# The zeros for unit 2's k and v change engines, and with them the place in the load queue that waits

## The chip, the cores and the metric

The kernel runs on one core of one Trainium2 chip. The metric is the device time of one execution in microseconds. Five engines run side by side, each with its own instruction stream: PE (matrix products, with a separate row PEld for its weight loads), DVE, ACT, POOL, and SP, which here only issues DMA transfers. SP issues them strictly in program order; an issue that must wait for a semaphore holds up every issue behind it.

## The reference

Eight batches, eight heads, 576 positions, head width 64. First an attention without a score matrix, then a layer that sends 128 of the 576 rows of each batch through an MLP:

```python
q_s = softmax(q over the head width);  k_s = softmax(k over the positions)
kv  = einsum('bhsd,bhse->bhde', k_s, v)
x   = einsum('bhsd,bhde->bhse', q_s, kv)        # heads side by side: (8, 576, 512)

scores = x @ w_gate
for each batch b:
    top = the 128 rows with the highest scores
    h   = max(x[b, top] @ w1, 0)                # 512 -> 1024
    out[b, top] = x[b, top] + sigmoid(scores[b, top]) * (h @ w2)
all other rows: out = x
```

## The kernel before

The attention is done in 16 **units**: unit u is four heads of one batch, two units to a batch. For a unit, ACT takes the exponential of k (`k_exp`, L235, tile `ke`) and of q (`q_exp`, L243, tile `qe`), an engine copies v beside a column of ones (`v_copy`, L247, tile `v_ones`; for unit 2 on POOL, for unit 3 on DVE), PE multiplies them (`kv_mm`, L259), DVE scales the result (`kv_out`), PE transposes q (`q_t`, L289 and L296), ACT or DVE brings it back (L299, L301), PE makes the rows of x (`x_mm`, L321), and DVE scales them (`x_scale`, L339). The scores of a batch are ranked on DVE (`compare`, L389), the 128 rows are found, and the MLP follows (L501 is its first product, in `mlp1`, L510 its second). For batch 0 the rows are not fetched from memory but picked by PE out of the tile that DVE has just written (`select`, L455); the picked rows come back through one copy on ACT (`turned`, L482, tile `xT`), and `mlp1` of batch 0 reads that copy.

The order of the whole program is written out by hand, so each engine's stream is the order of the calls. Raw k, v and q have three buffers each (`LD = 3`), so units 0, 1 and 2 load into fresh buffers and unit 3 takes over unit 0's.

A load of a unit's k or v is two transfers, because the 576 positions are split over 128 partitions, 5 rows to an even partition and 4 to an odd one. `load` (L108) first issues the transfer for the odd partitions (4 rows, 256 KB), then the one for the even partitions (5 rows, 320 KB). The fifth row of the odd partitions is never loaded; a fresh buffer needs zeros there. The zeros are written over the fifth row of all 128 partitions, so the second transfer of the pair writes over part of them and must wait until they are in place; the first does not touch them and does not wait. A load of q is two transfers of 288 KB.

At the start SP issues the loads of units 0 and 1, then unit 2's k, then unit 2's v and q, then w1 in four transfers (L145), then unit 3's k, v and q. POOL writes the zeros of unit 1's k and v and of unit 2's k right after its constants (L207). The zeros of unit 2's v are written by DVE, behind its copy of unit 0's transposed q (L299) and ahead of its half of unit 1's v copy (L793):

```python
q_t(0, 0, on_vector=True)
nc.vector.memset(raw["v"][2][:, :, N2], 0.0)
load(2, "vq")
load_w1(0)
```

Of the kernel before, what the change touches and what calls it, by code (L numbers as in the profile page):

```python
# [17 lines left out]
def kernel(  # L18
# [23 lines left out]
    nc = tc.nc  # L42
# [4 lines left out]
    N2 = R - 1  # L47
# [43 lines left out]
    def place(b):  # L91
        return (b - 1) % B
# [4 lines left out]
    def rows_of(b, upward):  # L97
# [7 lines left out]
    raw = {w: [const.tile([P, 2, T, D] if w == "q" else [P, 4, R, D], F32, name=f"{w}{n}") for n in range(LD)]  # L105
           for w in "qkv"}

    def load(u, which, queues=(nc.sync, nc.sync)):  # L108
        b, qd = units[u]
        for what in which:  # L110
            src = {"q": q, "k": k, "v": v}[what]
            t = raw[what][u % LD]
            first = src[place(b), 4 * qd].offset
            if what == "q":
                for h in range(2):
                    queues[h].dma_start(out=t[:, h].rearrange("p r d -> p (r d)"),
                                        in_=bass.AP(tensor=src.tensor, offset=first + 2 * h * SD,
                                                    ap=[[T * D, P], [1, T * D]]))
                continue
            for n, rows in ((1, N2), (0, R)):  # L120
                queues[n].dma_start(
                    out=t[n::2, :, :rows].rearrange("p h r d -> p h (r d)"),
                    in_=bass.AP(tensor=src.tensor, offset=first + n * R * D,
                                ap=[[T * D, 64], [SD, 4], [1, rows * D]]))
# [16 lines left out]
    def load_w1(half):  # L141

        c = slice(half * F // 2, (half + 1) * F // 2)
        for d in range(0, KD, 2):
            nc.sync.dma_start(out=w1[:, d:d + 2, c],  # L145
                              in_=moe_w1[d * P:(d + 2) * P, c].rearrange("(d p) f -> p d f", p=P))
# [56 lines left out]
    whole = const.tile([P, B * R], I32, name="whole")  # L203
    rest = const.tile([P, B * R], I32, name="rest")
    nc.gpsimd.iota(whole.rearrange("p (b r) -> p b r", b=B), pattern=[[S, B], [1, R]], base=0, channel_multiplier=T)
    for n, what in ((1, "k"), (1, "v"), (2, "k")):
        nc.gpsimd.memset(raw[what][n][:, :, N2], 0.0)  # L207
    load(1, "kvq")
    load(2, "k")
    vals = const.tile([P, B, R, NV], BF16, name="vals")  # L210
    valid_r = const.tile([P, 3, R], F32, name="valid_r")
    s_all = const.tile([P, B, R], F32, name="s_all")
# [63 lines left out]
    def q_t(u, c, on_vector=False, wide=False):  # L276

        if c == 0:
            st["qT", u] = at.tile([P, 2, R, 2, D], F32, tag="qT", name="qT", bufs=1)
        qe = st["qe", u] if c == 0 else st.pop(("qe", u))  # L280
        r0, r1 = ROWS[c]
        n = r1 - r0
        t_ps = ps.tile([P, 2, 512], F32, tag="x", name="x", bufs=2)
        to = st["qT", u][:, :, :n, c]
        if wide:
            to = to.rearrange("p a r t -> p r a t")
            src = t_ps.rearrange("p a c -> p (a c)")[:, :n * P]
            for r in range(n):
                nc.tensor.transpose(out=src[:, r * P:(r + 1) * P], in_=qe[:, r0 + r].rearrange("p i d -> p (i d)"),  # L289
                                    identity=ident)  # L290
            src = src.rearrange("p (r a t) -> p r a t", r=n, a=2)
        else:
            src = t_ps[:, :, :n * D].rearrange("p a (r t) -> p a r t", r=n)
            for r in range(n):
                for a in range(2):
                    nc.tensor.transpose(out=src[:, a, r], in_=qe[part(a), r0 + r].rearrange("p i d -> p (i d)"),  # L296
                                        identity=ident[part(a), part(a)])
        if on_vector:
            nc.vector.tensor_copy(out=to, in_=src)  # L299
        else:  # L300
            nc.scalar.copy(out=to, in_=src)  # L301
# [513 lines left out]
    fill(3)  # L815

    q_t(0, 0, on_vector=True)
    nc.vector.memset(raw["v"][2][:, :, N2], 0.0)
    load(2, "vq")
    load_w1(0)  # L820
    load_w1(1)
    q_t(0, 1)
# [305 lines left out]
```

## Time and profile before

| | |
|---|---|
| median of three runs | 199.6 us (199.15 to 199.66) |
| the profiled execution, its own time | 198.6 us |
| its span, first to last instruction | 196.9 us |
| PE busy | 185.4 us, 94% |
| DVE, ACT, POOL busy | 130.5, 102.7, 71.2 us |
| share of the chain that ended last: PE | 89% |
| share of the chain that ended last: DMA, DVE, ACT | 3%, 3%, 1% |
| moved by DMA | 46.68 MB, mean 237 GB/s |

All rows are of the one profiled execution; its own time is 1.7 us more than its span. Times inside it count from the start of the span. A row of the timeline gives start, duration, engine, line and operation, and in brackets how long the engine had been idle before and what ended that. A row that begins with SPq is a DMA issue: its duration is the time that SP takes to issue, not the time of the transfer. How long a transfer took from issue until it had landed is in the lists of DMA issues, where some engine waited for it.

### The profile page before, as it was taken

The numbers are of one execution on the slowest core, as the hardware profiler recorded it, in microseconds if no ns is written. First come the engines' busy times: TensorE is split into PE (matmuls) and PEld (weight loads), VectorE is DVE, ScalarE is ACT, GpSimd is POOL, SyncE is SP. The second block draws the span as 40 slices with busy tenths as digits, with TensorE's granted clock in tenths as the row PEclk, the third lists the DMA queues.
The fourth block names the chain that finished last, engine by engine and source line by source line (L and its number), as shares of the span: only waits on it lengthen the run. The fifth ranks groups of instructions, "written<-read, shape, count | busy, mean of one in ns | idle before, by whom it ended". The sixth has DMA issues, their size and how long they took to land.

```text
span 196.9 us, 7154 instructions
## 1 busy us (share of the span) xinstructions
PE 185.4 (94%) x2988; PEld 157.7 (80%) x2988; DVE 130.5 (66%) x423; ACT 102.7 (52%) x168; POOL 71.2 (36%) x126
## 2 busy tenths in 40 slices
PE   5799999999999999999999999999999999999950
PEld 2367799984679996679999988899999889898850
DVE  6376967493679659838997987289958955444010
ACT  3265543756597859848675858375433132312100
POOL 8022540201930490099706313145005354701230
PEclk9999999999999999999999999999999999999997
DMA  5999999999999999989968888938341414110011
GB/s 159 336 378 342 357 376 375 359 384 372 377 374 377 361 327 312 340 226 349 280 235 234 299 232 264 283 128 232 118 123 53 123 27 146 44 55 2 3 59 61
DMA packets 35210, 46.68 MB, mean 237 GB/s; under 512 B 2401, under 2 KB 28001, under 8 KB 35170
## 3 DMA queue, kind: packets, MB, share of 16 engines
q1 hardware_dynamic: 33616, 41.62, 64.8%
q0 software_dynamic: 1280, 4.20, 6.6%
q8 instruction: 25, 0.41, 0.8%
q10 hardware_dynamic: 274, 0.33, 0.5%
q14 instruction: 15, 0.12, 0.2%
HBM read 34.61 MB, written 11.53 MB: 234 GB/s over the span
## 4 chain that ended last, share of the span: by engine, by line
PE 89%; DMA 3%; DVE 3%; ACT 1%; issue 1%; POOLq 0%; POOL 0%; DVEq 0%
PE mm L594 19%; PE mm L646 19%; PE x L321 11%; PE tp L259 11%; PE mm L501 8%; PE mm L510 7%; PE x L296 5%; DMA v<-in_v_dram 3%; PE mm L455 2%; PE tp L378 2%; PE x L476 2%; DVE qT L299 1%; PE x L289 1%; PE mm L800 1%; PE tp L414 0%
## 5 line engine op out<-in xcount | busy, mean ns | idle before, releaser
L389 DVE SCALAR_TENSOR_TENSOR junk<-srow,s,stairs 128x576 bf16<-128x576 f32 x40 | 35.9, 897 | 1.3 <-ACT srow L381 0.5
L301 ACT COPY qT<-x 128x512 f32<-128x512 f32 (+1 forms) x30 | 17.9, 642 | 24.2 <-PE x L296 22.8
L339 DVE TENSOR_TENSOR xs<-x,qrec 128x640 f32<-128x640 f32 x32 | 25.2, 814 | 0.0
L439 POOL DMA_INDIRECT xr<-out_dram,idx x8 | 8.1, 1011 | 45.2 <-DVE no L432 14.7
L243 ACT ACTIVATE qe<-q 128x640 f32<-128x640 f32 (+1 forms) x32 | 20.3, 688 | 7.4 <-DMA q<-in_q_dram 7.4
L259 PE MATMUL tp<-v_ones,ke 128*64 128x65 f32 x640 | 22.2, 224 | 1.4 <-DVE v_ones L247 1.2
L321 PEld LDWEIGHTS x<-kv_w,qT 64*64 64x64 f32 x1152 | 20.5, 134 | 3.7 <-ACT qT L301 1.2
L321 PE MATMUL x<-kv_w,qT 64*64 64x66 f32 x1152 | 22.8, 222 | 0.4 <-DVE qT L299 0.4
L235 ACT ACTIVATE ke<-k 128x1280 f32<-128x1280 f32 x16 | 20.4, 1276 | 4.4 <-DMA k<-in_k_dram 4.0
L259 PEld LDWEIGHTS tp<-v_ones,ke 128*64 128x64 f32 x640 | 20.0, 137 | 3.3 <-issue 1.9
L646 PE MATMUL mm<-w,hT 128*128 128x256 f32 x96 | 22.2, 380 | 0.0
L646 PEld LDWEIGHTS mm<-w,hT 128*128 128x128 f32 x96 | 17.8, 191 | 2.1
L594 PE MATMUL mm<-xT,w 128*128 128x128 f32 x144 | 17.5, 276 | 0.0
L646 PE MATMUL mm<-tw,hT 128*128 128x256 f32 (+1 forms) x80 | 17.5, 363 | 0.0
L501 PE MATMUL mm<-xT,w 128*128 128x128 f32 x128 | 17.2, 283 | 0.0
L594 PEld LDWEIGHTS mm<-xT,w 128*128 128x128 f32 x144 | 16.8, 192 | 0.1
L501 PEld LDWEIGHTS mm<-xT,w 128*128 128x128 f32 x128 | 15.2, 192 | 0.8
L510 PE MATMUL mm<-w,hT 128*128 128x512 f32 x32 | 15.6, 611 | 0.0
L655 POOL TENSOR_TENSOR o<-o,xr 128x256 f32<-128x256 f32 x9 | 6.8, 757 | 23.7 <-ACT o L654 23.7
L646 PEld LDWEIGHTS mm<-tw,hT 128*128 128x128 f32 x80 | 13.8, 190 | 1.9 <-DVE o L659 0.3
L247 ACT COPY v_ones<-v 128x1280 f32<-128x1280 f32 x12 | 15.1, 1260 | 0.0
L332 DVE RECIPROCAL qrec<-x 128x10 f32<-128x10 f32 x32 | 7.0, 218 | 10.0 <-PE x L321 9.3
(146 smaller groups left out, 304.6 us busy)
## 6 DMA issues: line engine op xcount, KB each, us to landing
q<-in_q_dram SPq DMA_DIRECT2D x32, 288.0 KB, 5.9
v<-in_v_dram SPq DMA_DIRECT2D x16, 320.0 KB, 5.8
out_dram<-xs SPq DMA_DIRECT2D x16, 320.0 KB, 5.9
k<-in_k_dram SPq DMA_DIRECT2D x15, 320.0 KB, 7.6
k<-in_k_dram SPq DMA_DIRECT2D x16, 256.0 KB, 5.3
v<-in_v_dram SPq DMA_DIRECT2D x16, 256.0 KB
out_dram<-xs SPq DMA_DIRECT2D x16, 256.0 KB, 5.4
w<-in_moe_w_dram SPq DMA_DIRECT2D x4, 512.0 KB, 7.3
```

What stands on the lines that cost most here:

```text
L235: nc.scalar.activation(out=ke, in_=raw["k"][u % LD], func=AF.Exp)
L243: nc.scalar.activation(out=st["qe", u][:, r0:r1], in_=qr[:, r0:r1], func=AF.Exp)
L247: copy(out=v_ones[:, :, :, :D], in_=raw["v"][u % LD])
L259: nc.tensor.matmul(out=kv[part(h), i], lhsT=ke[:, 2 * h + i, r], rhs=vo[:, 2 * h + i, r], start=(r == 0), stop=(r == N2))
L301: nc.scalar.copy(out=to, in_=src)
L321: nc.tensor.matmul(out=to[:, r * C:(r + 1) * C], lhsT=lhsT, rhs=kw[part(i), a], start=True, stop=True)
L339: nc.vector.tensor_mul(xs[b][:, :, qd, :, a].rearrange("p r i d -> p i r d"), x[:, :, :, :D], rec.to_broadcast([P, 2, R, D]))
L389: nc.vector.scalar_tensor_tensor(junk, st["srow", b], st["s", b][:, r:r + 1], not_before[r], op0=OP.subtract, op1=OP.is_ge, accum_out=st[" ...
L501: nc.tensor.matmul(out=h_ps[:, f % HT * m:(f % HT + 1) * m], lhsT=w1[:, d, f * P:(f + 1) * P], rhs=xT[:, d, :m], start=(d == 0), stop=(d = ...
L510: nc.tensor.matmul(out=st["y", b][:m], lhsT=st["hT", b][:, f // HT, f % HT, :m], rhs=w2[:, f], start=(f == 0), stop=(f == KF - 1))
L594: nc.tensor.matmul(out=out_ps[:, f * m:(f + 1) * m], lhsT=w[:, k, f * P:(f + 1) * P], rhs=x()[:, k], start=first and f == 0 and k == 0, st ...
L646: nc.tensor.matmul(out=ps_of[to][:m, c:c + step], lhsT=st["hT", a][:, n, f, :m], rhs=w[:, f, c:c + step], start=first and f == 0, stop=f = ...
```

## The change

The two sets of zeros for unit 2 change places. POOL writes those of unit 2's v at the start instead of those of unit 2's k, and DVE writes those of unit 2's k behind unit 0's transposes instead of those of v. Unit 2's k, whose load was issued with unit 1's, is issued in one call with v and q, which stands behind DVE's zeros in the program.

```diff
-    for n, what in ((1, "k"), (1, "v"), (2, "k")):
+    for n, what in ((1, "k"), (1, "v"), (2, "v")):
         nc.gpsimd.memset(raw[what][n][:, :, N2], 0.0)
     load(1, "kvq")
-    load(2, "k")
...
     q_t(0, 0, on_vector=True)
-    nc.vector.memset(raw["v"][2][:, :, N2], 0.0)
-    load(2, "vq")
+    nc.vector.memset(raw["k"][2][:, :, N2], 0.0)
+    load(2, "kvq")
     load_w1(0)
```

On SP the order of the transfers stays as it was. This is the place in its stream from the last transfer of unit 1's q to the loads of unit 2's q, with what each issue waits for (k_81 and v_84 are unit 2's buffers; a DMAHW wait is for the landing of an earlier transfer; Pool and DVE are the zeros):

```order
 L116 DMA q_77<-in_q_dram 128x576 [waits DMAHW4_49]
 L121 DMA k_81<-in_k_dram 64x4x256 [waits DMAHW5_49]
-L121 DMA k_81<-in_k_dram 64x4x320 [waits DMAHW6_49,Pool_49]
-L121 DMA v_84<-in_v_dram 64x4x256 [waits DMAHW7_49]
-L121 DMA v_84<-in_v_dram 64x4x320 [waits DMAHW0_49,DVE_49]
+L121 DMA k_81<-in_k_dram 64x4x320 [waits DMAHW6_49,DVE_49]
+L121 DMA v_84<-in_v_dram 64x4x256 [waits DMAHW7_49]
+L121 DMA v_84<-in_v_dram 64x4x320 [waits DMAHW0_49,Pool_49]
 L116 DMA q_78<-in_q_dram 128x576 [waits DMAHW1_49]
```

The issue that waits for DVE's zeros is now two transfers further ahead: the second transfer of unit 2's k instead of the second of its v.

## Rows read from the trace of the kernel before

**Rows 1.** The page, its part on the chain of work that ended last: the share of the span by engine.
```profile
PE 89%; DMA 3%; DVE 3%; ACT 1%; issue 1%; POOLq 0%; POOL 0%; DVEq 0%
```

**Rows 2.** The waits of PE from 27 us to the end of the span, all that the view has: who waited for whom, us in total, times, longest.
```profile
PE mm L594 <- DVE xc L567: 0.3, 1, 0.3
```

**Rows 3.** The timeline of SP: the two transfers of unit 2's k, the two of its v; and, after the dots, the second transfer of unit 3's k.
```profile
8.94 0.61 SPq L121 DMA_DIRECT2D k<-in_k_dram  x1
9.70 0.61 SPq L121 DMA_DIRECT2D k<-in_k_dram  x1
10.38 0.60 SPq L121 DMA_DIRECT2D v<-in_v_dram  x1
13.03 0.60 SPq L121 DMA_DIRECT2D v<-in_v_dram  x1
...
18.66 0.76 SPq L121 DMA_DIRECT2D k<-in_k_dram  x1
```

**Rows 4.** The timeline of DVE: the zeros of unit 2's v, the first compare of batch 0, the copy of unit 3's v.
```profile
12.73 0.27 DVE L818 MEMSET v<- 128x256 f32 x1
...
21.66 0.82 DVE L389 SCALAR_TENSOR_TENSOR junk<-srow,s,stairs 128x576 bf16<-128x576 f32 x1
...
29.30 0.83 DVE L247 COPY v_ones<-v 128x1280 f32<-128x1280 f32 x1 [1.42 <-DMA v<-in_v_dram]
```

**Rows 5.** Stretches of the span from the first byte to 15 us: busy time of each engine, granted TensorE clock (1.00 is 2.4 GHz), DMA share, GB/s. No byte is moved before 2 us.
```profile
2.00:13.00 11.00, 9.35 (x91) 4.37 (x95) 6.03 (x34) 4.87 (x7) 2.74 (x7) 1.00 0.98 333
13.00:13.50 0.50, 0.50 (x48) 0.50 (x44) 0.47 (x1) 0.50 (x1) 0.42 (x1) 1.00 1.10 364
13.50:15.00 1.50, 1.50 (x56) 1.01 (x50) 1.32 (x6) 0.88 (x2) 0.60 (x1) 1.00 1.13 355
```

**Rows 6.** The page, its part on DMA issues: size of one transfer, median us from issue to landing.
```profile
q<-in_q_dram SPq DMA_DIRECT2D x32, 288.0 KB, 5.9
v<-in_v_dram SPq DMA_DIRECT2D x16, 320.0 KB, 5.8
...
k<-in_k_dram SPq DMA_DIRECT2D x16, 256.0 KB, 5.3
```

**Rows 7.** The timeline of SP: the first transfer of the program, and two issues later in it that came when the queue had run low.
```profile
0.81 0.76 SPq L121 DMA_DIRECT2D k<-in_k_dram  x1
...
102.51 0.63 SPq L350 DMA_DIRECT2D out_dram<-xs  x1
...
121.50 0.63 SPq L350 DMA_DIRECT2D out_dram<-xs  x1
```

**Rows 8.** Stretches of 0.25 us behind those issues, columns as in rows 5.
```profile
2.75:3.00 0.25, 0.25 (x2) 0.10 (x1) 0.25 (x3) 0.20 (x1) 0.25 (x1) 1.00 0.46 143
3.00:3.25 0.25, 0.25 (x2) 0.05 (x1) 0.25 (x1) 0.25 (x1) 0.25 (x1) 1.00 1.05 348
...
103.50:103.75 0.25, 0.25 (x5) 0.25 (x4) 0.25 (x1) 0.00 (x0) 0.25 (x1) 1.00 0.00 0
103.75:104.00 0.25, 0.25 (x5) 0.25 (x4) 0.03 (x1) 0.19 (x1) 0.24 (x2) 1.00 0.66 164
...
122.00:122.25 0.25, 0.25 (x3) 0.22 (x2) 0.00 (x0) 0.25 (x2) 0.25 (x1) 1.00 0.50 181
...
122.75:123.00 0.25, 0.25 (x3) 0.22 (x2) 0.00 (x0) 0.00 (x0) 0.25 (x1) 1.00 0.76 197
```

**Rows 9.** DMA issues of three short stretches (0 to 1 us, 11 to 13.6 us, 18.7 to 19.4 us), one transfer each: the first transfer of the program, the second of unit 2's v, the second of unit 3's k; size, us to landing.
```profile
k<-in_k_dram SPq DMA_DIRECT2D x1, 256.0 KB, 3.3
...
v<-in_v_dram SPq DMA_DIRECT2D x1, 320.0 KB, 4.7
...
k<-in_k_dram SPq DMA_DIRECT2D x1, 320.0 KB, 9.0
```

**Rows 10.** The timeline of ACT: the exponentials of unit 2's k and q and of unit 3's k, the copy of batch 0's picked rows, the exponentials of unit 3's q.
```profile
17.40 1.27 ACT L235 ACTIVATE ke<-k 128x1280 f32<-128x1280 f32 x1
...
21.43 1.26 ACT L243 ACTIVATE qe<-q 128x640 f32<-128x640 f32 x2
...
27.70 1.27 ACT L235 ACTIVATE ke<-k 128x1280 f32<-128x1280 f32 x1 [2.60 <-DMA k<-in_k_dram]
28.88 0.57 ACT L482 COPY xT<-mm 128x512 f32<-128x512 f32 x1
...
31.23 1.26 ACT L243 ACTIVATE qe<-q 128x640 f32<-128x640 f32 x2 [1.79 <-DMA q<-in_q_dram]
```

**Rows 11.** The timeline of PE: the product of unit 0's k and v, that of unit 2's, the first product of batch 0's MLP, the product of unit 3's k and v, the transposes of unit 3's q.
```profile
9.26 0.36 PE L259 MATMUL tp<-v_ones,ke 128*64 128x65 f32 x5 [1.23 <-DVE v_ones L247]
...
20.84 1.39 PE L259 MATMUL tp<-v_ones,ke 128*64 128x65 f32 x40
...
29.64 2.26 PE L501 MATMUL mm<-xT,w 128*128 128x128 f32 x16
31.83 1.39 PE L259 MATMUL tp<-v_ones,ke 128*64 128x65 f32 x40
33.15 0.78 PE L296 MATMUL x<-ident,qe 64*128 64x64 f32 x18
```

**Rows 12.** The timeline of POOL: the copy of unit 2's v, and the first step on batch 0's scores.
```profile
17.94 1.25 POOL L247 COPY v_ones<-v 128x1280 f32<-128x1280 f32 x1 [3.84 <-DVE qT L299]
20.18 0.20 POOL L361 TENSOR_TENSOR s<-s_all,valid_r 128x5 f32<-128x5 f32 x1 [0.98 <-DVE s_all L359]
```

## The prediction

> **What bounds the kernel now.** I read the chain of work that ended last first, since it says which engine carries the end: 89% of the span is PE [rows 1]. Then the waits of PE: from 27 us to the end there is one, of 0.3 us [rows 2]. So PE is full for the last 170 us, and whatever makes PE late by some time near 30 us comes out at the end whole; no later gap is there to take it up. The question is therefore narrow: does the change make PE late before or around 30 us, and by how much? The change touches only loads and zeros, so the next views are SP's stream [rows 3], the stretches with their GB/s [rows 5], and then, for each load that gets later, who reads it and when [rows 10 to 12].
>
> In the stretches the DMA is the busy thing: from the first byte at 2 us it moves 333 GB/s up to 13 us and 355 to 364 behind that, at a DMA share of about 1 [rows 5]. Loads come in one queue in one order, so a load is late by what the stream ahead of it lost. ACT does wait for it: unit 3's k exponential starts at 27.70 after 2.60 us idle, released by a DMA [rows 10]. The transfer it waits for was issued at 18.66 [rows 3] and took 9.0 us [rows 9]: landed at 27.66. That is the place at which a late stream is felt.
>
> **The change part by part.** *The zeros.* One memset on POOL and one on DVE stay one each, of the same shape; the row of DVE's is 0.27 us [rows 4]. Cost nothing; no other work is moved on either engine.
>
> *The wait on SP.* In the kernel before, SP issues both transfers of unit 2's k at 8.94 and 9.70 and the first of its v at 10.38; the second of its v needs DVE's zeros, which end at 12.73 + 0.27 = 13.00, and it goes out at 13.03 [rows 3, 4]. SP stands still from 10.98 to 13.03, 2.05 us. With the change the second transfer of k has that wait: SP stands still from 9.55 to 13.03, 3.48 us, and what is queued behind it is unit 2's v and q, w1, unit 3's k, v and q, and all later loads. Two transfers, 320 KB of k and 256 KB of v [rows 6], are thus issued 3.3 us later; everything behind them is late at SP by two issue times, 1.2 us. What counts is not SP but whether the DMA engines run out of bytes.
>
> *Do they run dry?* Bytes issued up to and with the first transfer of unit 2's k: two units of k, v and q, each 256 + 320 + 256 + 320 + 288 + 288 = 1728 KB [rows 6], and 256 KB: 3712 KB, which is 3.80 MB. Bytes moved by 13.00: 333 GB/s x 11 us = 3.66 MB; the remaining 0.14 MB takes 0.38 us at 364 GB/s [rows 5]. So the engines are out of work at 13.38 on the mean. In the kernel before, 0.59 MB more was in the queue there, enough at 355 to 364 GB/s until 15.0, and the transfer issued at 13.03 was in time; that stall of SP cost nothing.
>
> *When do bytes flow again?* The issue comes at 13.03. The nearest rows are two later issues at a queue that had run low: issued at 102.51, nothing moved up to 103.75 and 164 GB/s in the next quarter; issued at 121.50, down to 181 GB/s at 122.00 to 122.25 while the old work ran out, and back to 197 from 122.75 [rows 7, 8]. Both are 1.25 us from issue to bytes. So bytes flow from 14.28, and the stream has lost 14.28 - 13.38 = 0.90 us. The cold start is the upper bound: issued at 0.81, still 143 GB/s in the quarter before 3.00 and 348 behind it [rows 7, 8]; 2.2 us, which here means 15.2 and a loss of 1.85 us. The lower bound is no loss, for engines that are still busy when the new work comes. I take 0.90 us, since the two later rows are of a running program.
>
> The Trainium skill's page "DMA: Bandwidth & Descriptors", section "Specifications", gives about 0.6 us to the first byte of a transfer issued from SP, where the rows above show 1.25. By the page the loss would be an estimated 0.25 us, PE would be late by 0.1, and the median would come out at 199.7; the sum goes by the rows.
>
> *Who feels 0.9 us.* Unit 2's k: issued at 13.03 into an empty queue, 3.3 us (the first transfer of the program) to 4.7 us (the one issued at 13.03 now) to landing [rows 9], so 16.3 to 17.7. Its exponential starts at 17.40 now; even if it starts at 17.8 it ends at 19.1, 1.7 us before PE's product at 20.84 needs it [rows 10, 11]. Covered. Unit 2's v lands at 13.03 + 4.7 = 17.73 now; POOL copies it at 17.94 for 1.25 us [rows 9, 12]. At 0.9 us later it ends at 20.1, ahead of the same product at 20.84 and of POOL's own next step at 20.18: covered, with 0.1 us to spare on POOL and another 1.0 us before DVE's compare at 21.66 [rows 4, 12] needs that step's result. Unit 2's q is read at 21.43 with no wait shown [rows 10], and w1 lies ahead of unit 3's k in the queue and is read only behind it. Covered.
>
> Unit 3's k is not. ACT starts its exponential at 27.70 when it lands, and right behind it in ACT's stream stands the copy of batch 0's picked rows, 28.88 to 29.45; PE's first MLP product reads that copy and starts at 29.64 [rows 10, 11]. With k 0.9 us later the exponential starts at 28.60, the copy runs from 29.78 to 30.35, and PE, some 0.05 us behind it, starts at 30.40 instead of 29.64. The slack was 0.14 us, so **0.76 us, say 0.8**, is lost on PE. The copy itself has its data by then; it is late because it is queued on ACT behind a load that is late.
>
> The two behind it are hidden in that: unit 3's v, copied on DVE from 29.30 (also waiting for DMA), would end at 31.0 against a product at 31.83 + 0.8; unit 3's q exponentials, from 31.23 for 1.26 us, would end at 33.4 against transposes at 33.15 + 0.8 [rows 4, 10, 11]. A pause of PE of 0.8 us does not bring the clock down as far as this trace tells: PE idled 1.23 us before 9.26 [rows 11], and the granted clock of that stretch is 1.00, its 2.4 GHz level [rows 5].
>
> *The sum.* Span 196.9 + 0.8 = 197.7 us; the profiled execution 198.6 + 0.8 = 199.4 us; the median of the runs, which lies 1.0 us above the profiled execution, 199.6 + 0.8 = **200.4 us**.
>
> **The rivals.** *First, the last engines never run dry (not slower).* Its place is the queue between 13.0 and 14.3, its price nothing, and its point is 0.14 us: a loss at unit 3's k below that is taken up by the slack at PE's 29.64. What speaks for it: the engines do not run out together. At 122 us the rate falls from 181 GB/s over at least half a microsecond [rows 8], so those that are behind have work to about 0.5 us past the mean, 13.9, and lose 0.4 us; and a transfer has landed only when the last of its engines is done. If the same ones are still last at unit 3's k, the loss there is 0.4 us or less and PE's 0.25 or less. That gives 199.6 to 199.9 us. Against it: nothing shows that the same engines stay last over the 14 us in between.
>
> *Second, a quick restart.* If bytes flow within 0.5 us of the issue at 13.03, the loss is 13.53 - 13.38 = 0.15 us, no more than PE's slack, and the median stays at 199.6. Both later issues speak against it with 1.25 us [rows 7, 8]; for it, only that they were stores and no loads. The page of the Trainium skill named above comes close to it.
>
> *Third, the restart is as slow as at the start.* Loss 1.85 us, PE late by 1.85 - 0.14 = 1.7 us: 201.3 us. Unit 2's v would then end its copy near 21.0, 0.2 us past PE's 20.84, and POOL's scores step would reach DVE's compare just in time, so that place would still add nothing. For it speaks only the cold first transfer [rows 7, 8]; against it, both later issues.
>
> *Fourth, faster.* Nothing on PE's path gets shorter: no load is issued earlier and no instruction goes. It could only be engines that fall into step after running dry, so that later transfers land sooner; PE waits for none of them now [rows 2], so even that buys nothing. What is left is the scatter.
>
> **How the numbers follow.** Forecast 200.4 us: 0.54. First rival, 199.6 to 199.9: 0.26. Second, 199.6: 0.06. Third, 201.3: 0.10. Faster: 0.04. The range goes from 199.5, which takes in the first two rivals and a little scatter, to 201.3, the upper bound of the loss. A measurement of this kernel can tell about 0.3%, or 0.6 us, from no change. The forecast lies only 0.2 us beyond that, so of its 0.54 some 0.12 falls below the line: slower by over 0.3% has 0.42 + 0.10, and with a little scatter from the first rival 0.53; within 0.3% has 0.12 + 0.26 + 0.06 less that scatter, 0.43; faster 0.04.
>
> **What would show it.** In the profile of the changed kernel SP should issue one transfer of unit 2's k near 8.9, the next near 13.0, and unit 2's v behind that. The GB/s should fall in the quarters between 13.2 and 14.3; if they stay above 340 the engines never ran dry and the first rival holds. The exponential of unit 3's k should start near 28.6, the copy of the picked rows end near 30.35, and PE's first MLP product start near 30.4 after a wait for ACT; the product of unit 2's k and v should still start near 20.8. It is wrong if PE waits anywhere before that product, if unit 3's k lands by 27.8 in spite of a gap, or if PE's delay at 30 us is not found again in the span.

## The result, and the profile after

The changed kernel takes 201.28 us at the median of 19 runs, the kernel before 199.46 us at the median of 19 runs beside it. The ratio is 1.0095 with a 95% interval of 1.0068 to 1.0121: 1.9 us slower (0.0095 x 199.46), where 0.8 us slower was forecast. The range of 199.5 to 201.3 just holds it. The profiled execution of the changed kernel took 201.28 us, with a span of 199.6 us; that of the kernel before, 198.6 us, lies 0.9 below its median here, so the two traces differ by more than the medians do.

The place is the one forecast. This is the waits of PE in the changed kernel, from 9 us to the end: who waited for whom, us in total, times, longest.

```profile
PE mm L500 <- ACT xT L481: 2.3, 1, 2.3
...
PE mm L593 <- DVE xc L566: 0.3, 1, 0.3
```

The second row is the one that the kernel before has too [rows 2]; the rows left out are 1.2 us or less in total each, and stand in the first 21 us but for one pause of 0.29 us at 151.74. The first is new: PE's first MLP product waits 2.3 us for the copy of the picked rows on ACT. The timeline of ACT in the changed kernel around it, and of PE:

```profile
17.07 1.27 ACT L234 ACTIVATE ke<-k 128x1280 f32<-128x1280 f32 x1
...
29.89 1.27 ACT L234 ACTIVATE ke<-k 128x1280 f32<-128x1280 f32 x1 [5.11 <-DMA k<-in_k_dram]
31.06 0.57 ACT L481 COPY xT<-mm 128x512 f32<-128x512 f32 x1
```

```profile
20.51 1.39 PE L258 MATMUL tp<-v_ones,ke 128*64 128x65 f32 x40
...
31.68 2.05 PE L500 MATMUL mm<-xT,w 128*128 128x128 f32 x16 [2.30 <-ACT xT L481]
```

Unit 3's k exponential starts at 29.89 instead of 27.70, the copy stands right behind it, and PE starts at 31.68 instead of 29.64 [rows 10, 11]: 2.04 us late. Unit 2 is not touched: its exponential starts at 17.07 and its product at 20.51, both 0.33 us earlier than before, as this execution's first product was (8.94 instead of 9.26). Of the 2.7 us by which the span grew, the new wait accounts for some 2: the next product of PE, that of unit 3's k and v, is 1.83 us late (33.66 instead of 31.83 [rows 11]). The rest came later in the execution, 0.29 us of it in the pause at 151.74.

Why k is so late stands in SP's timeline and the stretches of the changed kernel. SP's timeline has the two transfers of unit 2's k, the two of its v, and the second of unit 3's k; a stretch has busy time of each engine, granted clock, DMA share and GB/s.

```profile
8.68 0.61 SPq L121 DMA_DIRECT2D k<-in_k_dram  x1
12.70 0.61 SPq L121 DMA_DIRECT2D k<-in_k_dram  x1
13.36 0.62 SPq L121 DMA_DIRECT2D v<-in_v_dram  x1
14.07 1.50 SPq L121 DMA_DIRECT2D v<-in_v_dram  x1
...
19.46 0.94 SPq L121 DMA_DIRECT2D k<-in_k_dram  x1
```

```profile
12.50:13.00 0.50, 0.50 (x36) 0.50 (x40) 0.47 (x2) 0.50 (x1) 0.25 (x1) 1.00 1.05 375
13.00:13.25 0.25, 0.25 (x32) 0.25 (x26) 0.20 (x1) 0.25 (x1) 0.25 (x1) 1.00 0.80 273
13.25:13.50 0.25, 0.25 (x31) 0.25 (x24) 0.18 (x1) 0.25 (x1) 0.25 (x1) 1.00 0.36 122
13.50:13.75 0.25, 0.25 (x21) 0.21 (x12) 0.21 (x3) 0.08 (x1) 0.25 (x1) 1.00 0.20 71
13.75:14.00 0.25, 0.10 (x4) 0.11 (x2) 0.25 (x1) 0.00 (x0) 0.02 (x1) 1.00 0.14 49
14.00:14.25 0.25, 0.24 (x1) 0.00 (x0) 0.25 (x1) 0.07 (x1) 0.00 (x0) 1.00 0.95 185
14.25:14.50 0.25, 0.25 (x7) 0.18 (x8) 0.25 (x2) 0.25 (x1) 0.00 (x0) 1.00 0.88 97
14.50:14.75 0.25, 0.25 (x14) 0.25 (x14) 0.21 (x3) 0.25 (x1) 0.00 (x0) 1.00 0.46 123
14.75:15.00 0.25, 0.25 (x16) 0.25 (x13) 0.25 (x2) 0.25 (x2) 0.00 (x0) 1.00 0.96 328
...
15.00:16.00 1.00, 1.00 (x29) 0.93 (x24) 0.74 (x3) 0.44 (x1) 0.00 (x0) 1.00 1.05 362
16.00:16.50 0.50, 0.50 (x8) 0.33 (x8) 0.50 (x4) 0.01 (x1) 0.00 (x0) 1.00 0.70 145
16.50:17.00 0.50, 0.34 (x9) 0.27 (x8) 0.25 (x3) 0.50 (x1) 0.00 (x0) 1.00 0.60 76
17.00:17.50 0.50, 0.50 (x3) 0.19 (x2) 0.50 (x1) 0.50 (x2) 0.00 (x0) 1.00 0.88 313
...
13.00:15.50 2.50, 2.34 (x97) 2.01 (x88) 2.31 (x7) 1.84 (x3) 0.77 (x1) 1.00 0.68 196
15.50:20.50 5.00, 4.38 (x104) 3.10 (x102) 3.33 (x15) 1.86 (x2) 1.72 (x4) 1.00 0.92 299
```

The same two long stretches of the kernel before:

```profile
13.00:15.50 2.50, 2.50 (x106) 2.01 (x100) 2.29 (x7) 1.88 (x3) 1.02 (x1) 1.00 1.07 348
15.50:20.50 5.00, 4.70 (x115) 3.27 (x111) 3.33 (x14) 2.14 (x3) 1.50 (x3) 1.00 1.02 352
```

The engines run out behind 13.0 us, as worked out. But the stream does not come back whole 1.3 us after the issue at 12.70: bytes flow from 14.0, and the rate stays at 97 to 185 GB/s until 14.75. Then, after a good microsecond, it falls a second time, to 145 and 76 GB/s between 16 and 17. In sum the changed kernel moved (348 - 196) x 2.5 = 0.38 MB less up to 15.5 us and (352 - 299) x 5 = 0.27 MB less from there to 20.5 us. At 355 GB/s that is 1.07 and 0.75 us, together 1.8 us against a forecast of 0.90. Unit 3's k exponential is 2.19 us late (29.89 instead of 27.70), so some 0.4 us of its delay is not in this count and stays open.

### The profile page after: what moved, and what is told of

Read it like the earlier page. It is cut to its first block, busy times and chain, and to the rows that moved or that the text cites. A ratio compares the mean times of both kernels' runs of the same rounds, so it can differ in the third digit from the quotient of the medians.

```text
span 199.6 us, 7150 instructions
## 1 busy us (share of the span) xinstructions
PE 185.1 (93%) x2984; PEld 157.8 (79%) x2988; DVE 130.5 (65%) x423; ACT 102.8 (51%) x168; POOL 71.9 (36%) x126
## 4 chain that ended last, share of the span: by engine, by line
PE 80%; DMA 8%; SPq 3%; DVE 3%; ACT 2%; issue 1%; POOLq 0%; POOL 0%; ACTq 0%; DVEq 0%
PE mm L593 19%; PE mm L645 19%; PE tp L258 9%; PE x L320 9%; PE mm L500 8%; PE mm L509 7%; DMA k<-in_k_dram 5%; PE x L295 5%; DMA v<-in_v_dram 3%; PE tp L377 2%; PE x L475 2%; SPq L121 1%; SPq L145 1%; ACT ke L234 1%; ACT xT L481 1%
## 5 line engine op out<-in xcount | busy, mean ns | idle before, releaser
L320 PE MATMUL x<-kv_w,qT 64*64 64x66 f32 x1152 | 23.5, 222 | 0.7 <-DVE qT L298 0.4
L331 DVE RECIPROCAL qrec<-x 128x10 f32<-128x10 f32 x32 | 7.0, 217 | 11.0 <-PE x L320 10.2
```

Of the source, the lines that this page charges most:

```text
L320: nc.tensor.matmul(out=to[:, r * C:(r + 1) * C], lhsT=lhsT, rhs=kw[part(i), a], start=True, stop=True)
```

## The experiments

Eleven kernels ran. Ratios are to the kernel before on the same chip, with a 95% interval; an edit is shown against the changed kernel where nothing else is said. The theory was that SP's stop leaves the DMA engines without bytes, and that this is felt at unit 3's k because the copy of the picked rows is queued behind it on ACT. The rivals were that it matters that k itself is late or that DVE writes its zeros, and that the time goes elsewhere behind the dry stretch.

**DVE's zeros early.**

```diff
     ready(0)
     nc.vector.tensor_copy(out=wg.rearrange("p a i d -> p (a i d)"), in_=g_ps[:, :4 * D])
+    nc.vector.memset(raw["k"][2][:, :, N2], 0.0)
...
     q_t(0, 0, on_vector=True)
-    nc.vector.memset(raw["k"][2][:, :, N2], 0.0)
     load(2, "kvq")
```

> The changed kernel with one line moved: DVE writes the zeros of unit 2's k right behind its copy of wg (DVE is idle there, from 9.1 us on in the changed kernel's trace) instead of behind unit 0's transposes. The load and its place are untouched. Theory (SP's stop lets the DMA engines run dry, and unit 3's k, with the copy of the picked rows queued behind it on ACT, makes PE wait at 29 us): SP goes on near 9.7 us, no stretch between 12 and 18 us falls under 300 GB/s except by the instruction fetch near 14 us, PE's wait for that copy (2.30 us) is gone, median 199.2 to 199.8 us. Rival (it is not the stop but that the zeros of a k are DVE's and its load is called later): as the changed kernel, 201.0 to 201.6 us.

Measured: 200.33 us, ratio 1.0051 (1.0020 to 1.0083). The stop, the dry stretch and the wait for the picked rows are gone, and still only about half of the loss came back: a miss, as 199.2 to 199.8 us was expected. The timeline of PE shows what took its place: two pauses with nothing to wait for, one in the middle of a series of equal products.

```profile
18.56 0.62 PE L320 MATMUL x<-kv_w,qT 64*64 64x66 f32 x25 [0.99 <-issue]
...
24.83 0.38 PE L454 MATMUL mm<-hT,xs 128*128 128x128 f32 x2 [0.48 <-issue]
```

**Unit 2's v ahead of its k.**

```diff
-    load(2, "kvq")
+    load(2, "vkq")
```

> The changed kernel with unit 2 loaded in the order v, k, q instead of k, v, q; the zeros stay where the change put them. SP stops as long for DVE's zeros, but two more transfers (0.59 MB, 1.6 us of DMA work at 365 GB/s) are in the queue before it stops, as in the kernel before. Theory (bytes in the queue): no dry stretch near 13.5 us, PE's wait at 29 us gone, median 199.3 to 200.0 us; unit 2's k lands near 17.7 us, which its exponential and PE's product at 20.5 us allow. Rival (unit 2's k must not be late): k is still later than in the changed kernel, so 201.3 us or more.

Measured: 199.56 us, ratio 1.0016 (0.9990 to 1.0043). SP stops for DVE's zeros from 10.2 to 12.1 us, with two more transfers in the queue, and the stream does not notice:

```profile
9.63 0.61 SPq L121 DMA_DIRECT2D k<-in_k_dram  x1
12.13 0.60 SPq L121 DMA_DIRECT2D k<-in_k_dram  x1
```

```profile
13.00:15.50 2.50, 2.34 (x61) 1.94 (x53) 2.40 (x9) 1.26 (x3) 0.69 (x1) 1.00 1.08 361
15.50:20.50 5.00, 4.37 (x109) 3.12 (x110) 3.45 (x13) 2.39 (x3) 2.12 (x6) 1.00 1.06 388
```

361 and 388 GB/s, where the changed kernel has 196 and 299. DVE still writes the zeros of k, and the same transfer of k still waits for them: that rival falls.

**The copy of the picked rows ahead of unit 3's k on ACT.**

```diff
         if r == 0:
             q_t(2, 1)
-            k_exp(3)
+    k_exp(3)
     kv_out(2)
```

> The changed kernel with ACT's exponential of unit 3's k called behind the select of batch 0, so that the copy of the picked rows stands ahead of it on ACT; loads and zeros untouched. Theory (PE is late because that copy is queued behind a late load): the dry stretches stay, the copy ends near 28.5 us and PE's first MLP product starts near 29.1 us without a wait; what is left is a wait of PE for unit 3's v (copied by DVE until 32.4 us) at the product of unit 3's k and v, which would come at 31.3 us: about 1.1 us of the 2.3 stay, median 200.0 to 200.4 us. Rival (PE is late for something else behind the dry stretch, such as w1): 201.0 to 201.6 us.

Measured: 201.51 us, ratio 1.0126 (1.0097 to 1.0156): nothing came back, and the figure is the rival's, not the theory's. In the trace PE's wait for the copy is gone, and the product of unit 3's k and v starts at 32.36 instead of 33.66, but PE had stood still before that, again for nothing that is shown, at the same instruction as above:

```profile
24.26 0.38 PE L454 MATMUL mm<-hT,xs 128*128 128x128 f32 x2 [1.50 <-issue]
```

By itself this run neither supports nor refutes the place; the run with w1 below supports it.

**DVE's zeros late.** The zeros and the loads of unit 2 and w1 behind them are called 2 us later.

```diff
-    nc.vector.memset(raw["k"][2][:, :, N2], 0.0)
-    load(2, "kvq")
-    load_w1(0)
-    load_w1(1)
...
     x_scale(0, 0)
+    nc.vector.memset(raw["k"][2][:, :, N2], 0.0)
+    load(2, "kvq")
+    load_w1(0)
+    load_w1(1)
```

> The changed kernel with DVE's zeros, and the loads of unit 2 and w1 behind them, called 2 us later, behind the first scaling of unit 0's rows; SP would go on near 14.8 us instead of 12.7. If the loss were one dry stretch as long as SP's stop, all of the 2 us would be added: 203.3 us. If the changed kernel's loss is two parts, a dry stretch of 1.2 us and a second one of 0.8 us because the third issue after the stop took 1.50 us while a 16 KB instruction fetch ran at 14.1 us, the fetch now falls into the stop and its part drops out: a single stretch of about 2.7 us, unit 3's k some 0.8 us later than in the changed kernel, 201.8 to 202.4 us. Rival (the stop itself costs nothing): no change against the changed kernel, 201.3 us.

Measured: 203.12 us, ratio 1.0212 (1.0178 to 1.0247), 1.8 us more than the changed kernel by the medians and 2.3 us by the ratios. So the loss grows with the stop. My reading of the second slow stretch, as an effect of the 1.50 us issue at 14.07, falls: SP issues quickly here, and the stretch is there all the same, at 18 us. The place, too, has moved: unit 2's v is now so late that PE's product of unit 2 waits for POOL's copy.

```profile
23.40 2.30 PE L258 MATMUL tp<-v_ones,ke 128*64 128x65 f32 x40 [2.90 <-POOL v_ones L246]
```

```profile
17.00:18.00 1.00, 0.94 (x31) 0.62 (x34) 0.52 (x1) 0.10 (x1) 0.00 (x0) 1.00 1.07 382
18.00:19.00 1.00, 0.96 (x62) 0.93 (x54) 0.39 (x2) 0.81 (x1) 0.00 (x0) 1.00 0.82 182
...
24.00:25.00 1.00, 1.00 (x24) 1.00 (x22) 0.96 (x4) 0.75 (x2) 0.94 (x2) 0.50 1.06 406
```

The last row also shows a granted clock of 0.50, the 1.2 GHz level, behind PE's pause of 2.90 us. So a part of this run's loss is the clock's, and its time is no clean measure of 2 us of stop. The stream is: it moved 70 and 222 GB/s from 13.00 to 15.50 and from 15.50 to 20.50 us, which by the same count is a loss of 3.8 us. That is 2.0 us more than in the changed kernel, and SP went on 1.99 us later (14.69 instead of 12.70).

**DVE's zeros one instruction earlier.**

```diff
+    nc.vector.memset(raw["k"][2][:, :, N2], 0.0)
     q_t(0, 0, on_vector=True)
-    nc.vector.memset(raw["k"][2][:, :, N2], 0.0)
     load(2, "kvq")
```

> The changed kernel with DVE's zeros one instruction earlier, ahead of its copy of unit 0's transposes instead of behind it: SP would go on some 0.8 us earlier, near 11.9 us, and bytes flow near 13.2 us, when the engines run out. A point on the curve between the early zeros (SP stops 0.1 us, ratio 1.0051) and the changed kernel (1.0095). Theory (loss by the dry stretch): no dry stretch, no wait of PE near 29 us, 199.3 to 200.0 us. If the second slow stretch, seen behind the dry one at 16 to 17 us in the changed kernel, belongs to any restart with a short queue: 0.8 us of stream is still lost, 200.0 to 200.6 us. Rival (the stop's length does not matter): 201.3 us.

Measured: 198.75 us, ratio 0.9973 (0.9939 to 1.0006). The whole loss is regained. The trace is less simple than the time: SP goes on 1.68 us earlier (unit 2's second k transfer is issued at 11.02, not 12.70, where about 0.8 us was forecast; 0.54 us of it is this execution's earlier start, PE's first product at 8.40 instead of 8.94). The dry stretch is gone, a slow one is not (270 and 319 GB/s in the two long stretches, a loss of 1.0 us), and PE still waits 1.17 us for the picked rows.

```profile
13.00:14.00 1.00, 1.00 (x28) 0.51 (x18) 0.97 (x4) 0.28 (x2) 0.34 (x1) 1.00 1.11 342
14.00:15.00 1.00, 1.00 (x40) 1.00 (x36) 0.96 (x3) 1.00 (x2) 0.00 (x0) 1.00 0.95 262
15.00:16.00 1.00, 1.00 (x17) 0.76 (x15) 0.75 (x5) 0.08 (x2) 0.00 (x0) 1.00 0.73 143
16.00:17.00 1.00, 1.00 (x12) 0.42 (x8) 0.75 (x3) 0.64 (x1) 0.00 (x0) 1.00 0.78 262
```

```profile
30.35 2.05 PE L500 MATMUL mm<-xT,w 128*128 128x128 f32 x16 [1.17 <-ACT xT L481]
```

**All zeros on POOL.**

```diff
-    for n, what in ((1, "k"), (1, "v"), (2, "v")):
+    for n, what in ((1, "k"), (1, "v"), (2, "k"), (2, "v")):
         nc.gpsimd.memset(raw[what][n][:, :, N2], 0.0)
...
-    nc.vector.memset(raw["k"][2][:, :, N2], 0.0)
     load(2, "kvq")
```

> The changed kernel with all four sets of zeros on POOL and none on DVE, so SP never stops for zeros of unit 2. Two readings of the early-zeros run, which lost 1.0 us against the kernel before without any dry stretch. If it lost because the queue is always full and PE's own instructions, fetched in 16 KB pieces through the same DMA engines, come late (in its trace a piece began at 16.1 us instead of 14.8 and PE stood still twice, 1.1 and 0.5 us, with nothing to wait for): here too, 200.0 to 200.8 us, and again two such pauses of PE between 17 and 26 us. If it lost because DVE's zeros stood in front of its first kv_out: gone here, 199.0 to 199.7 us.

Measured: 199.82 us, ratio 1.0028 (1.0003 to 1.0054). SP never stops for unit 2's zeros and nothing is gained on the kernel before. The pauses of PE are there again, 0.84 and 0.20 us at the same two instructions. The time lies between the two forecasts. The pauses do not come from DVE's zeros; whether a smaller part of the first run's loss does is not shown, since the intervals of the two runs overlap.

```profile
18.67 0.62 PE L320 MATMUL x<-kv_w,qT 64*64 64x66 f32 x25 [0.84 <-issue]
...
25.07 0.38 PE L454 MATMUL mm<-hT,xs 128*128 128x128 f32 x2 [0.20 <-issue]
```

**The second half of w1 behind unit 3's loads.**

```diff
     load_w1(0)
-    load_w1(1)
...
     load(3, "kvq")
+    load_w1(1)
```

> The changed kernel with the second half of w1 (1 MB, 2.9 us of stream) loaded behind unit 3's k, v and q instead of ahead of them; zeros, stop and ACT's order as in the changed kernel. Theory (the late stream is felt at unit 3's k, with the copy of the picked rows behind it): the dry stretches stay, unit 3's k lands by 27.3 us, PE's wait of 2.3 us near 29 us is gone; PE reads the late half of w1 only near 33.5 us. 199.3 to 200.1 us. Rival (the time goes elsewhere behind the dry stretch, in PE's late instruction pieces or unit 2's v): 200.8 to 201.6 us.

Measured: 199.65 us, ratio 1.0021 (0.9982 to 1.0060). The stream is as poor as in the changed kernel, 251 and 275 GB/s in the two long stretches (0.63 MB less than in the kernel before, where the changed kernel moved 0.65 MB less), but unit 3's k lands earlier, its exponential starts at 26.80, and PE does not wait there:

```profile
13.00:15.50 2.50, 2.50 (x97) 2.01 (x86) 2.41 (x7) 1.81 (x3) 0.85 (x1) 1.00 0.86 251
15.50:20.50 5.00, 4.70 (x107) 3.10 (x101) 3.33 (x15) 1.89 (x4) 1.48 (x3) 1.00 0.81 275
```

```profile
26.80 1.27 ACT L234 ACTIVATE ke<-k 128x1280 f32<-128x1280 f32 x1 [2.04 <-DMA k<-in_k_dram]
27.98 0.58 ACT L481 COPY xT<-mm 128x512 f32<-128x512 f32 x1
```

```profile
29.30 2.05 PE L500 MATMUL mm<-xT,w 128*128 128x128 f32 x16
```

That is the cleanest test of where the loss is felt: the holes stay, the time comes back. One wait is left in this trace: at 48.06 us PE waits 0.87 us for a copy that stands on ACT behind a later k.

**The same move in the kernel before.** The edit is that of the last run.

> The kernel before with the same move of the second half of w1. PE does not wait for unit 3's k in the kernel before, so by the theory nothing is gained: 199.1 to 199.7 us. If the kernel before too loses time at unit 3's k in many of its runs (its runs scatter from 198.4 to 201.8), the median falls below 199.0 us and the scatter narrows.

Measured: 199.01 us, ratio 0.9993 (0.9960 to 1.0026). No gain, as expected by the theory; the figure lies just below its 199.1 to 199.7 us.

**Unit 2's q between its k and v.**

```diff
-    load(2, "kvq")
+    load(2, "kqv")
```

> The changed kernel with unit 2 loaded in the order k, q, v instead of k, v, q: two transfers of q stand where those of v stood, behind the stop. Meant for the trace: behind the dry stretch the changed kernel has a second slow one at 16 to 17 us (about 100 GB/s), when the third transfer behind the stop, the second of unit 2's v, begins. If any third transfer behind a stop is slow (the queue has no lead), the stretch stays near 15.9 us, now in q; if it is the v transfer, it moves behind q, to 17.5 us or later. The time is no test: v lands 1.6 us later, near 21 us, POOL's copy then ends near 22.5 us and PE's product of unit 2, at 20.5 us in the changed kernel, waits some 2 us. 201.5 to 203.5 us.

Measured: 203.25 us at the median of four runs, which scatter from 200.59 to 204.56; ratio 1.0121 (1.0043 to 1.0200). The time is that of a late v, and no test. The stretches answer the question with both: the stream is slow in q, near 16 us, and again in v, near 18 us.

```profile
14.50:15.50 1.00, 1.00 (x26) 0.93 (x22) 0.97 (x3) 0.78 (x2) 0.00 (x0) 1.00 1.07 394
15.50:16.50 1.00, 1.00 (x13) 0.50 (x11) 0.74 (x6) 0.61 (x2) 0.00 (x0) 1.00 0.93 217
16.50:17.50 1.00, 0.94 (x32) 0.63 (x34) 0.50 (x1) 1.00 (x2) 0.00 (x0) 1.00 1.01 369
17.50:18.50 1.00, 1.00 (x62) 0.92 (x52) 0.41 (x3) 0.25 (x1) 0.00 (x0) 1.00 0.69 198
```

So the second slow stretch does not belong to one transfer. In the changed kernel, in that with late zeros and in that with half of w1 later the rate falls when 0.54 to 0.59 MB have moved since the bytes came back (by 16.00, 18.25 and 16.25 us), which is about what the first two transfers behind the stop hold (576 KB, or 0.59 MB). Which property of a restarted queue makes it is open.

**Both recoveries together.** DVE's zeros one instruction earlier, and the second half of w1 later.

> Both edits that recovered the loss each by itself: DVE's zeros of unit 2's k ahead of its copy of the transposes (198.75 us by itself), and the second half of w1 behind unit 3's loads (199.65 us by itself). Theory: in the trace of the first, PE still waited 1.17 us near 30 us for the copy of the picked rows behind unit 3's k; with k 2.9 us of stream earlier that wait goes, 198.0 to 198.8 us. If what is left there is hidden in most runs, no change: 198.5 to 199.2 us.

Measured: 199.31 us beside 199.71 us of the kernel before, ratio 0.9972 (0.9947 to 0.9997). That is no better than the zeros alone (0.9973), and both stretches expected, in us, were missed; the kernel before is itself slower beside this run (199.71) than beside those of the two edits (199.19). The interval ends just under one, so at most a small gain on the kernel before is shown.

**The kernel before with its zeros one instruction earlier.**

```diff
+    nc.vector.memset(raw["v"][2][:, :, N2], 0.0)
     q_t(0, 0, on_vector=True)
-    nc.vector.memset(raw["v"][2][:, :, N2], 0.0)
     load(2, "vq")
```

> The kernel before with DVE's zeros of unit 2's v one instruction earlier, ahead of its copy of unit 0's transposes, so that SP's stop for them is 0.8 us shorter. By the bytes in the queue that stop cost nothing, so no gain: 199.0 to 199.6 us. If the restart behind it costs something (the 310 and 250 GB/s near 15 and 17.5 us in the trace of the kernel before), 198.4 to 198.9 us. By the reading of the full queue (PE's instruction pieces come later when SP stops less) it could even be 199.5 to 200.0 us.

Measured: 200.46 us, ratio 1.0039 (1.0009 to 1.0070): slower than all three forecasts, with a shorter stop of SP. PE pauses 0.40 and 0.48 us at the two instructions where it pauses in the run with early zeros. But the longest wait of this trace is another: at 75.21 us PE waits 1.31 us for the fetched rows of a later batch (tile `xr`, a DMA), for which the trace of the kernel before shows no wait. So how much of the loss is the shorter stop's is not shown.

## Why the prediction was right and wrong

**Right: the direction, the chain and the place.** The zeros themselves cost nothing. The engines ran out of bytes behind 13.0 us (13.38 was worked out), PE started every product before 29 us as early as before, and its one new wait for another engine is for the copy of the picked rows behind unit 3's k. Two runs show it from two sides: with two more transfers queued ahead of the wait for the same zeros the loss is gone (1.0016), and with the holes left in but unit 3's k moved ahead of 1 MB of w1 it is gone, within its interval (1.0021). With SP going on 1.68 us earlier it is gone too (0.9973), though that trace still has a stream loss of 1.0 us and a wait of 1.17. Against it stands the copy moved ahead of unit 3's k (1.0126): there PE stood still at another place, with nothing waited for, and no time came back. The covers named for unit 2's k, v and q held. Unit 2's v was named as the next to be late, and at a longer stop it is (2.90 us of PE's time in the run with late zeros).

**Wrong: one term of the sum.** The step that failed reads "the stream has lost 14.28 - 13.38 = 0.90 us". It took the first byte, 1.25 us behind the start of the issue, for the return of the whole rate. The changed kernel shows the first byte where it was expected, 1.3 us behind the issue at 12.70, but then three quarters at 97 to 185 GB/s and a second fall to about 110 GB/s between 16 and 17 us. Measured by bytes the loss is 1.07 us up to 15.5 and 0.75 us behind it, 1.8 us. Less the 0.14 us of slack that would be 1.7 us on PE; the trace has 2.04, the runs 1.9.

The cold start, with 143 GB/s in the last quarter before 3.00 [rows 8], was taken as an upper bound at 0.10. The whole rate did come back as late as it has it, 2.05 us behind the issue (14.75) where the cold start took 2.2. But that its 1.85 us of loss and its 201.3 us are nearly what came is luck: the restart itself lost 1.07 us, and the second fall, 0.75 us, is in no rival. The two later issues were given more weight because they were of a running program, but both were stores, and behind both only the first byte was used. The trace of the kernel before goes on at 139 to 217 GB/s from 103.75 to 105.50, and at 152 to 229 from 122.75 to 124.50; how much of that is the restart and how much the stores, it does not show.

**The other rivals.** The first rival had its premise right and its price wrong. The engines did not run out together: the rate falls over a whole microsecond, from 273 to 49 GB/s, and all that had been issued has moved only by 14.0, when new bytes come. Yet the loss at unit 3's k was not 0.4 us or less, but 2.19. The quick restart is refuted as it was counted, from the start of the issue: 1.3 us, not 0.5. From the end of the issue, which takes 0.61 us, it is 0.69 us, and 0.61 and 0.62 behind the two stores [rows 7, 8], in stretches of 0.25 us. The stop of the kernel before was said to cost nothing; that holds, since neither shortening it (1.0039) nor removing it altogether (1.0028) gained anything.

## What to carry to other kernels

Here a wait in front of a load cost nothing that shows as long as the bytes still queued outlasted it (1.0016 with two more transfers queued), and beyond that by its length (2.0 us of stream for 1.99 us of stop). So count what has been issued and not yet moved, and put the waiting transfer behind enough of it. When the queue does run dry, charge more than the time to the first byte; here the stream lost 1.8 us where the gap to the first byte was 0.9. And look for the reader with the least slack, however far downstream: a copy that was ready stood on ACT behind an exponential whose load was late, and loading other data later than that k repaired the time without touching the gap.

## What was not expected of the hardware

**PE pauses with nothing to wait for, and more often when the DMA queue is always full.** In eight of the eleven experiments PE pauses at one or both of the same two instructions, the first of them in the middle of a series of equal products: at the first only with no stop of SP or a shorter one (0.99, 0.84 and 0.40 us), at the second also in kernels whose queue ran low (up to 1.50 us). Shorter pauses of the kind, 0.2 to 0.5 us, stand later in several traces, near 38, 50, 112 and 150 us. The page counts 25 packets and 0.41 MB of instructions on one DMA queue in the kernel before, 16 KB each, and the lists of DMA queues in short stretches say when a piece moves. In the kernel with early zeros pieces begin in the stretches 16.00 to 16.25 and 22.25 to 22.50 us; PE goes on at 18.56 and 24.83, some 2.4 us later each time. With the copy of the picked rows first, a piece begins at 21.75 to 22.00 and PE goes on at 24.26; with v first, at 21.00 to 21.25, and PE goes on at 23.57. In the kernel before the piece that answers to the first begins earlier, at 14.75 to 15.00, and PE does not pause. This is the list of DMA queues in that stretch of the kernel before: packets, MB, share of the 16 engines' time.

```profile
q1 hardware_dynamic: 71, 0.07, 109.1%
q8 instruction: 1, 0.02, 28.7%
```

I read this as PE's own instructions, which come through the same DMA engines and wait behind queued data. No run took the pieces away, so it is argued and not shown; it fits that three kernels with no stop or a shorter one (1.0051, 1.0028, 1.0039) are slower than the kernel before although SP holds no transfer back for long in them, but the last of them has the wait of 1.31 us at 75 us as well. It doesn't explain why the kernel with its zeros one instruction earlier is as fast as it is (0.9973): there PE pauses 0.20 us at the second of the two and still waits 1.17 us for the picked rows. Part of the answer is that one trace is one execution: PE's first product starts at 8.40 us there and at 9.26 in the kernel before, and over all thirteen traces between 8.15 and 9.26, ahead of the loads that the edits move. That is as much as most of the effects here, so single spans can't be set against each other. Where that kernel makes its time good in the median of twelve runs is open.

**The clock fell behind one pause of PE and not behind another.** Behind PE's 2.30 us in the changed kernel the granted clock stays at 1.00; behind 2.90 us in the kernel with late zeros it is 0.50, the 1.2 GHz level, from 24 to 27 us, and with a pause of 3.50 us, up to 23.48, in the kernel with q before v it is 0.50 from 23 to 26.
